# Halves of a batch's queries of 256 and 320 tokens instead of 320 and 256

## The chip, the cores and the metric

The kernel runs on one core of a Trainium2 chip. The metric is the device time of one execution in microseconds, the median of the runs that were timed.

## What is computed

Three layers follow each other. The first is attention with 4 batches, 8 heads, 576 tokens a batch and 64 numbers a head. It has two parts that are added: every query sees the keys less than 4 positions away (local), and the mean of 4 neighbouring queries sees the 144 means of 4 neighbouring keys (pooled), its output being repeated for the 4 tokens:

```python
out_d = sm_attn(q_d, k_d, v_d)               # means of 4 tokens, 144 a batch
out_up = np.repeat(out_d, factor, axis=2)
mask = np.abs(pos[:, None] - pos[None, :]) < factor
...
return (out_up + out_local).astype(np.float32)
```

The second layer is dense, over 2304 tokens of 512 numbers: `h = x @ w_in; g = h * cos(h); x = g @ w_out`, with 2048 hidden numbers. The third routes each token to the best of 8 experts (512 to 1024 to 512 with a relu) and scales by the softmax of the gate.

## The kernel before

**Attention.** A batch's 576 queries are nine tiles of 64. Two heads (a head pair, hp = 0 to 3) are worked on together, one in partitions 0 to 63 and one in 64 to 127. `HALF` (line 72) cuts the 576 queries in two: for each half the first group of 4 tokens, the number of groups, and the groups in one pooled product. So the first half has 80 groups, that is 320 tokens or five tiles, and its pooled queries go in two products of 40; the second has 64 groups, that is 256 tokens or four tiles, in one product of 64. `QROWS` gives the shape in which the queries are loaded.

`queries` (line 152) does one half of one head pair in seven steps, with a `yield` behind each: transposes of the queries (tq, L128, L165 to L169); local scores with a mask and their exponentials p (L178 to L191; a tile of 64 queries sees a window of 70 keys); pooled scores and their exponentials pd (L200 to L207); transposes of p (pt, L214); transposes of pd and, where there is a fifth tile, of its p (ptd, L222 to L229); pooled output (o, L234, L237); local output (L245), the sum of both (xo, L247), and a sink that takes it on. `together` runs several of these generators in turn, one step each. In batch 0 the four head pairs of the first half run together, then the four of the second; in batches 1 to 3 the two halves of each head pair do.

**Handing over.** `first_x` (line 297) is the sink in batch 0: it cuts the tokens of a half at the blocks of 256 and writes each piece as a rounded part xh (L306, ScalarE) and a rest xl (L307; VectorE for the first half, GpSimd for the second) into the blocks x[0] and x[1], and what lies beyond token 512 goes to the DRAM tensor xT through SP's queue (L311). All other batches go through xT (L264 to L282), and `load_x` brings blocks 2 to 8 back.

**The dense layer.** Tokens go in nine blocks of 256. `hidden(i, fp)` (L379) makes 256 hidden numbers of block i, with 24 matmuls of rounded and rest parts, then `h * cos(h)` on ScalarE and VectorE (L385 to L393); `project(i, fp)` (L407) adds them into the block's output. The float64 weights are loaded as words by SP (L329), joined on VectorE (L339 to L343), and split on ScalarE (L348) and GpSimd (L350) by `convert_w`. The weights (fp, 0) are for `hidden`, (fp, 1) for `project`.

**Order.** The program's text gives priorities, and a scheduler plans the order on each engine from them before the run. The first half of batch 0 runs first, with three conversions among its steps; xo is held behind the joining of the last of them by `issue_after`. `hidden(0, 0)` and `hidden(0, 1)` follow. From there a list of slots interleaves the dense layer with the rest of the attention: `marks` gives the step of the attention that is due at each slot. The second half of batch 0 is due by slot 1, ahead of the first hidden of block 1, `(1, 0)`. Steps are counted in yields, and each half has seven.

Of the kernel before, what the change touches and what calls it, by code (L numbers as in the profile page):

```python
# [10 lines left out]
BF16 = mybir.dt.bfloat16  # L11
# [8 lines left out]
P = 128  # L20
# [11 lines left out]
class Kernel:  # L32
# [18 lines left out]
    def constants(self):  # L51
        nc, pool = self.nc, self.const
        self.ident = pool.tile([P, P], F32, name="ident")
        nc.gpsimd.memset(self.ident, 0.0)
        nc.gpsimd.affine_select(out=self.ident, in_=self.ident, compare_op=ALU.not_equal, fill=1.0,
                                base=0, pattern=[[-1, P]], channel_multiplier=1)
        self.ident16 = pool.tile([P, P], BF16, name="ident16")
        nc.gpsimd.tensor_copy(self.ident16, self.ident)
        self.mask = pool.tile([P, 9, 70], BF16, name="mask")
        nc.gpsimd.memset(self.mask, 0.0)  # L60
        for half in range(2):
            for t0, t1, off in ((0, 1, 0), (1, 8, 3), (8, 9, 6)):
                m = self.mask[half * 64:(half + 1) * 64, t0:t1, :]
                pat = [[0, t1 - t0], [-1, 70]]
                nc.gpsimd.affine_select(out=m, in_=m, compare_op=ALU.is_ge, fill=NEG,
                                        base=off + 3, pattern=pat, channel_multiplier=1)
                nc.gpsimd.affine_select(out=m, in_=m, compare_op=ALU.is_ge, fill=NEG,
                                        base=3 - off, pattern=[[0, t1 - t0], [1, 70]], channel_multiplier=-1)

    HALF = ((0, 80, 40), (80, 64, 64))
    QROWS = ((80, 4), (128, 2))
    KROWS = ((96, 3), (96, 3))
    VHALF = ((0, 72), (72, 72))

# [9 lines left out]
    def lane(self, pool, engine, n):  # L86

        qs = []
        for j, (g0, ng, gq) in enumerate(self.HALF):
            qdbd = pool.tile([P, ng // gq, 2, gq], F32, name=f"qdbd{n}_{j}")  # L90
# [25 lines left out]
    def load_windows(self, b, h, j):  # L116

        g0, ng, _ = self.HALF[j]
        first = g0 // 16 + (1 if j == 0 else 0)
# [34 lines left out]
    def queries(self, pool, n, n_, j, qs, raw, hp, kd, kT, vd, vw, sink, behind=None):  # L154

        nc, S = self.nc, self.S
        qdbd = qs[j]
        g0, ng, gq = self.HALF[j]
        nt, nd, t0 = ng // 16, ng // gq, g0 // 16
# [3 lines left out]
        ps = self.psum([P, 320], f"tq_{n_}")  # L163
        self.turn(ps, raw, self.QROWS[j], hp)
        nc.scalar.mul(qT[:, :4 * ng], ps[:, :4 * ng], 0.125)  # L165
        nc.vector.tensor_reduce(out=qd[:, :ng], in_=ps[:, :4 * ng].rearrange("p (g f) -> p g f", f=4), axis=AX.X, op=ALU.add)
        for par in range(2):
# [7 lines left out]
        sm = pool.tile([P, 5], F32, tag="sm", bufs=n, name=f"sm_{n_}")  # L175
        p = pool.tile([P, 5, 70], F32, tag="p", bufs=max(n, 2), name=f"p_{n_}")
        ps = self.psum([P, 5, 70], f"s_{n_}")
        nc.tensor.matmul(ps[:, :nt, :], lhsT=self.ident16, rhs=self.mask[:, t0:t0 + nt, :], start=True, stop=False,  # L178
                         skip_group_check=True)
        for i in range(nt):  # L180
            w0 = min(max(64 * (t0 + i) - 3, 0), S - 70)
            for par in range(2):
                r = slice(64 * par, 64 * par + 64)
                nc.tensor.matmul(ps[r, i, :], lhsT=qT[r, 64 * i:64 * i + 64], rhs=kT[r, w0:w0 + 70],  # L184
                                 start=False, stop=(i == nt - 1), skip_group_check=True)
# [12 lines left out]
        ps = self.psum([P, 2, 144], f"sd_{n_}")  # L198
# [13 lines left out]
        ps = self.psum([70, 4, P], f"pt_{n_}")  # L212
# [4 lines left out]
        ps = self.psum([80, 512], f"ptd_{n_}")  # L217
# [13 lines left out]
        ps = self.psum([P, 512], f"o_{n_}")  # L231
        for kj, (k0, nk) in enumerate(self.VHALF):
            for par in range(2):
                nc.tensor.matmul(ps[64 * par:64 * par + 64, 320:320 + ng].rearrange("p (a b) -> p a b", a=nd), lhsT=vd(kj, par)[:nk],  # L234
                                 rhs=pdT[kj][:, :, gq * par:gq * par + gq], start=(kj == 0), stop=(kj == 1))
# [18 lines left out]
    def attention(self, pool, qs, b, hp):  # L254

        nc, S = self.nc, self.S
        n_ = f"{b}_{hp}"
        ks, vs = [], []
        for j, (r, n) in enumerate(self.KROWS):
            ks.append(pool.tile([P, 4, P], F32, tag="raw", bufs=self.RAWS, name=f"rawk{j}_{n_}"))  # L260
            self.load_rows(ks[j], self.k, b, hp, j * r * n, (r, n))
        for j, (g0, ng) in enumerate(self.VHALF):
            vs.append(pool.tile([P, 512], F32, tag="raw", bufs=self.RAWS, name=f"rawv{j}_{n_}"))
            nc.sync.dma_start(out=vs[j][:ng].rearrange("g (h c) -> g h c", h=2),  # L264
                              in_=self.v[b, 2 * hp:2 * hp + 2, 4 * g0:4 * (g0 + ng), :].rearrange("h (g f) d -> g h (f d)", f=4))
        yield
        for kd, kT in self.keys(pool, 1, ks, None, n_):
            yield
        vd = self.pooled_values(pool, 1, vs, 2, n_, nc.gpsimd)
        yield  # L270
        halves = []
        for j, (g0, ng, _) in enumerate(self.HALF):
            raw = pool.tile([P, 4, P], F32, tag="raw", bufs=self.RAWS, name=f"rawq{j}_{n_}")
            self.load_rows(raw, self.q, b, hp, 4 * g0, self.QROWS[j])
            vw = pool.tile([70, 5, 2, 64], F32, tag="vw", bufs=2, name=f"vw{j}_{n_}")
            edge, e0, i0 = (0, 0, 1) if j == 0 else (3, S - 70, 0)
            nc.sync.dma_start(out=vw[:, edge, :, :], in_=self.v[b, 2 * hp:2 * hp + 2, e0:e0 + 70, :].rearrange("h s d -> s h d"))
            for par in range(2):
                nc.sync.dma_start(out=vw[:, i0:i0 + ng // 16 - 1, par, :], in_=self.load_windows(b, 2 * hp + par, j))

            def sink(x, g0=g0, ng=ng):
                nc.sync.dma_start(out=self.xT[hp * P:(hp + 1) * P, b * S + 4 * g0:b * S + 4 * (g0 + ng)], in_=x[:, :4 * ng])  # L282

            halves.append(self.queries(pool, 2, n_, j, qs, raw, None, kd, kT, lambda kj, par: vd[kj][:, par, :],
                                       lambda i, par, vw=vw: vw[:, i, par, :], sink))
        yield
        yield from self.together(halves, 2)
# [11 lines left out]
    def first_x(self, x, hp, j):  # L299

        nc, TB = self.nc, self.TB
        at, done = 4 * self.HALF[j][0], 0
        while at < 2 * TB and done < 4 * self.HALF[j][1]:
            n = min(TB - at % TB, 4 * self.HALF[j][1] - done)
# [440 lines left out]
    def run(self):  # L745
        nc, tc, E, NT, KD = self.nc, self.tc, self.E, self.NT, self.KD
        S = self.S
# [31 lines left out]
        def load(nm, src, rows=None, j=0):  # L779
            raw[nm, j] = pr.tile([P, 2048], F32, tag="raw", name=f"raw{nm}{j}")  # L780
            if rows is None:
                self.load_pooled(raw[nm, j], src, 0, j)
            else:
                self.load_batch(raw[nm, j], src, 0, j * rows[0] * rows[1], rows)

        def windows(j):
            vw = pp.tile([70, 5, 8, 64], F32, tag="vw", name=f"vw{j}")
            ng = self.HALF[j][1]
            edge, e0, i0 = (0, 0, 1) if j == 0 else (3, S - 70, 0)
            nc.sync.dma_start(out=vw[:, edge, :, :], in_=self.v[0, :, e0:e0 + 70, :].rearrange("h s d -> s h d"))  # L790
            for h in range(8):
                nc.sync.dma_start(out=vw[:, i0:i0 + ng // 16 - 1, h, :], in_=self.load_windows(0, h, j))
            return vw

        for j in range(2):
            load("k", self.k, self.KROWS[j], j)
        load("q", self.q, self.QROWS[0])
        self.constants()
        pool = self.const
# [35 lines left out]
        for hp in range(4):  # L835
            for got in self.keys(pp, 4, [raw["k", j] for j in range(2)], hp, f"0_{hp}"):
                pass
            kv.append(got)
        vw = windows(0)
        for w in early[1:]:  # L840
            self.load_w(*w)
# [4 lines left out]
        def first(hp, j):  # L846
            if j == 0:
                q, at = raw["q", 0], hp
            else:
                q, at = ap.tile([P, 4, P], F32, tag="raw", bufs=self.RAWS, name=f"rawq_{hp}"), None  # L850
                self.load_rows(q, self.q, 0, hp, 4 * self.HALF[1][0], self.QROWS[1])
            yield from self.queries(pp, 4, f"0_{hp}", j, lanes[hp], q, at, *kv[hp],
# [11 lines left out]
        self.hbanks = [psh]  # L864
        self.abanks = [banks, self.psx]
        vw = windows(1)
        raws.close()
        att = ExitStack()
# [200 lines left out]
```

## Time and profile before

| | |
|---|---|
| median of 3 runs | 896.86 us (890.33 to 897.53) |
| profiled execution | 899.56 us, span of its trace 897.4 us |
| TensorE matmul busy | 837.3 us, 93% |
| VectorE busy | 540.8 us, 60% |
| ScalarE busy | 506.9 us, 56% |
| GpSimd busy | 203.1 us, 23% |
| mean granted TensorE clock | 0.956 of 2.4 GHz |

The span runs from the first to the last instruction of the profiled execution; its time has the launch around it as well. A busy share is a mean over the whole span, and stages differ.

### The profile page before, as it was taken

What the parts mean: (1) busy time and instruction counts of PE and PEld (TensorE: products, weight loads), DVE (VectorE), ACT (ScalarE), POOL (GpSimd) and SP (SyncE); (2) the same over time, 40 slices, a digit from 0 to 9 for tenths busy, and PEclk for the clock granted to TensorE, in tenths of its full rate; (3) what the DMA queues carried; (4) which work ended last, traced back from release to release, by engine and by line L of the source; (5) the groups of instructions that cost most, each with busy time, mean ns of one, the idle gap of its engine ahead of it and who ended that gap; (6) DMA issues with size and microseconds to landing.
All of it is one profiled execution on the core that took longest, in us unless ns stands there. A gap on an engine that the chain in (4) does not pass through costs nothing.

```text
span 897.4 us, 16850 instructions
## 1 busy us (share of the span) xinstructions
PE 837.3 (93%) x6114; PEld 724.6 (81%) x6114; DVE 540.8 (60%) x1331; ACT 506.9 (56%) x1278; POOL 203.1 (23%) x296
## 2 busy tenths in 40 slices
PE   6779897999899999899999999999899999999995
PEld 5577776878787888788888989898779888888894
DVE  5874789854634467585574848587455654555420
ACT  4657766777557576656744444475255644545421
POOL 4544345341221222221201010110222022012200
PEclk9579889899989999999999999999999999999998
DMA  9822925223415222332010000052548655455110
GB/s 200 266 70 60 334 67 165 58 69 91 101 42 148 68 56 59 70 80 71 1 37 25 26 25 24 31 160 71 150 133 299 224 174 174 163 171 193 58 37 22
DMA packets 112730, 95.89 MB, mean 107 GB/s; under 512 B 65152, under 2 KB 92876, under 8 KB 112636
## 3 DMA queue, kind: packets, MB, share of 16 engines
q1 hardware_dynamic: 108524, 83.96, 32.0%
q0 software_dynamic: 4112, 10.76, 4.0%
q8 instruction: 50, 0.82, 0.4%
q14 instruction: 44, 0.36, 0.1%
HBM read 81.31 MB, written 13.98 MB: 106 GB/s over the span
## 4 chain that ended last, share of the span: by engine, by line
PE 70%; DMA 8%; DVE 7%; issue 6%; ACT 5%; POOL 3%; SPq 1%; POOLq 0%; DVEq 0%; ACTq 0%
PE h L379 19%; PE acc L407 19%; PE eacc L655 10%; PE eph L636 9%; DMA lists<-tokens,posi 2%; PE s L184 2%; PE o L234 2%; DMA xT<-xo 1%; DMA raw<-in_moe_w_dram 1%; PE sd L200 1%; PE o L245 1%; PE ptd L222 1%; DVE w L343 1%; DMA out_dram<-y,ids 1%; PE tq L128 1%
## 5 line engine op out<-in xcount | busy, mean ns | idle before, releaser
L379 PE MATMUL h<-xh,w 128*128 128x256 f32 x1152 | 236.6, 294 | 8.1 <-POOL w L350 3.6
L379 PEld LDWEIGHTS h<-xh,w 128*128 128x128 f32 x1152 | 190.5, 196 | 12.9 <-POOL w L350 4.2
L407 PE MATMUL acc<-w,gh 128*128 128x512 f32 x576 | 194.9, 412 | 0.0
L379 PE MATMUL h<-xl,w 128*128 128x256 f32 x576 | 167.9, 292 | 1.4 <-DVE xl L307 1.4
L407 PEld LDWEIGHTS acc<-w,gh 128*128 128x128 f32 x576 | 105.2, 192 | 19.9 <-ACT gh L392 0.3
L636 PE MATMUL eph<-exh,w 128*128 128x256 f32 (+5 forms) x512 | 117.8, 306 | 0.0
L407 PE MATMUL acc<-w,gl 128*128 128x512 f32 x288 | 116.8, 406 | 0.4 <-DVE gl L393 0.4
L379 PEld LDWEIGHTS h<-xl,w 128*128 128x128 f32 x576 | 112.7, 196 | 4.0 <-DVE xl L307 1.6
L564 DVE TENSOR_TENSOR w<-raw,w 128x512 fp32r<-128x512 f32 x128 | 83.4, 688 | 32.0 <-ACT w L563 31.4
L655 PE MATMUL eacc<-w,hh 128*128 128x512 f32 (+4 forms) x304 | 99.2, 407 | 1.0 <-ACT hh L644 1.0
L636 PEld LDWEIGHTS eph<-exh,w 128*128 128x128 f32 x512 | 87.8, 190 | 3.3
L563 ACT CAST w<-raw 128x512 fp32r<-128x512 f32 x128 | 73.7, 619 | 28.4 <-DMA raw<-in_moe_w_dram 15.0
L385 ACT ACTIVATE u<-h 128x512 int32<-128x512 f32 x72 | 43.3, 601 | 70.9 <-PE h L379 70.7
L636 PE MATMUL eph<-exl,w 128*128 128x256 f32 (+5 forms) x256 | 78.6, 307 | 0.0
L389 DVE SCALAR_TENSOR_TENSOR u<-u,h 128x512 f32<-128x512 f32 x72 | 49.3, 685 | 48.4 <-ACT u L388 48.0
L386 DVE SCALAR_TENSOR_TENSOR u<-h,u 128x512 f32<-128x512 f32 x72 | 49.3, 685 | 37.7 <-ACT u L385 37.2
L455 DVE SCALAR_TENSOR_TENSOR prod<-row,wgb 128x512 f32<-128x512 f32 x96 | 66.4, 691 | 6.5 <-ACT row L449 5.0
L483 POOL DMA_INDIRECT lists<-tokens,posi x18 | 19.3, 1074 | 210.5 <-DVE posi L480 205.2
L392 ACT CAST gh<-u 128x512 fp32r<-128x512 f32 x72 | 44.8, 622 | 36.7 <-DVE u L389 20.5
L407 PEld LDWEIGHTS acc<-w,gl 128*128 128x128 f32 x288 | 55.0, 191 | 12.4 <-DVE gl L393 0.9
L393 DVE TENSOR_TENSOR gl<-u,gh 128x512 fp32r<-128x512 f32 x72 | 52.0, 723 | 20.6 <-ACT gh L392 20.3
L387 ACT ACTIVATE u<-u 128x512 f32<-128x512 f32 x72 | 45.5, 631 | 30.3 <-DVE u L386 30.1
(178 smaller groups left out, 1442.5 us busy)
## 6 DMA issues: line engine op xcount, KB each, us to landing
raw<-in_moe_w_dram SPq DMA_DIRECT2D x64, 512.0 KB
f<-in_moe_w_in_dram SPq DMA_DIRECT2D x8, 1024.0 KB
f<-in_moe_w_out_dram SPq DMA_DIRECT2D x8, 1024.0 KB
rows<-row SPq DMA_DIRECT2D x9, 520.0 KB
xraw<-xT SPq DMA_DIRECT2D x14, 256.0 KB
rawk<-in_k_dram SPq DMA_DIRECT2D x48, 72.0 KB
rawv<-in_v_dram SPq DMA_DIRECT2D x24, 144.0 KB
vw<-in_v_dram SPq DMA_DIRECT2D x32, 70.0 KB
```

Of the source, the lines that this page charges most:

```text
L379: nc.tensor.matmul(ph[:, fo, :], lhsT=a[:, kk, f], rhs=b[:, kk, :], start=(n == 0), stop=(n == 3 * self.KD - 1))
L386: nc.vector.scalar_tensor_tensor(out=u, in0=hv, scalar=1.0 / (2 * math.pi), in1=turns, op0=ALU.mult, op1=ALU.subtract)
L387: nc.scalar.activation(u, u, AF.Sin, scale=PI)
L389: nc.vector.scalar_tensor_tensor(out=u, in0=u, scalar=1.0, in1=hv, op0=ALU.subtract, op1=ALU.mult, reverse0=True)
L392: nc.scalar.copy(gh, u)
L393: nc.vector.tensor_tensor(out=gl, in0=u, in1=gh.bitcast(F32), op=ALU.subtract)
L407: nc.tensor.matmul(self.acc[i][t], lhsT=a[:, fo, t * P:(t + 1) * P], rhs=b[:, fo, :], start=(f == 0 and n == 0), stop=(f == self.NF - 1 an ...
L455: nc.vector.scalar_tensor_tensor(out=prod, in0=row[:, t, :DM], scalar=1.0, in1=self.spread[e // 2][:, e % 2, :], op0=ALU.mult, op1=ALU.mul ...
L563: nc.scalar.copy(hi, raw[:, sl])
L564: nc.vector.tensor_tensor(out=lo, in0=raw[:, sl], in1=hi.bitcast(F32), op=ALU.subtract)
L636: self.lastmm = nc.tensor.matmul(ph, lhsT=a[:, kk, f % 2 * P:(f % 2 + 1) * P], rhs=b[:, kk, :cols], start=(n == 0), stop=(n == 3 * self.KD ...
L655: self.lastmm = nc.tensor.matmul(self.eacc[w][:m], lhsT=a[:, at * P:at * P + m], rhs=b[:, f % 2, :], start=(f == 0 and n == 0), stop=(f == ...
```

## The change

The two halves change their sizes. The first half of every batch has 64 groups, so 256 tokens, four tiles, one pooled product of 64; the second has 80 groups, 320 tokens, five tiles, two pooled products of 40. The queries' load shapes change places with them. The mask held one pattern for each of the nine tiles, of which the seven inner ones are alike; it now holds six, and a half takes its own from place 0 or 1 on. The window at the end of the sequence stands in place 4 of the second half's five. `first_x` is not edited, but its cuts now fall elsewhere: the first half is block 0 and nothing else, and the second is block 1 and 64 tokens for xT.

```diff
-        self.mask = pool.tile([P, 9, 70], BF16, name="mask")
+        self.mask = pool.tile([P, 6, 70], BF16, name="mask")
...
-            for t0, t1, off in ((0, 1, 0), (1, 8, 3), (8, 9, 6)):
+            for t0, t1, off in ((0, 1, 0), (1, 5, 3), (5, 6, 6)):
...
-    HALF = ((0, 80, 40), (80, 64, 64))
-    QROWS = ((80, 4), (128, 2))
+    HALF = ((0, 64, 64), (64, 80, 40))
+    QROWS = ((128, 2), (80, 4))
...
-        nc.tensor.matmul(ps[:, :nt, :], lhsT=self.ident16, rhs=self.mask[:, t0:t0 + nt, :], start=True, stop=False,
+        nc.tensor.matmul(ps[:, :nt, :], lhsT=self.ident16, rhs=self.mask[:, j:j + nt, :], start=True, stop=False,
...
-            edge, e0, i0 = (0, 0, 1) if j == 0 else (3, S - 70, 0)
+            edge, e0, i0 = (0, 0, 1) if j == 0 else (4, S - 70, 0)
```

The last pair of lines stands twice in the kernel, in `attention` and in `windows`.

## Rows read from the trace of the kernel before

**Rows 1.** Stretches of 20 us: length, then busy us (instructions) of each engine, clock, DMA.

```profile
20.00:40.00 20.00, 13.47 (x112) 9.76 (x112) 18.82 (x50) 14.11 (x61) 8.19 (x9) 0.58 0.97 308
40.00:60.00 20.00, 13.77 (x109) 12.94 (x107) 16.84 (x33) 10.33 (x22) 9.64 (x7) 0.67 0.27 62
...
480.00:500.00 20.00, 20.00 (x132) 17.92 (x131) 12.12 (x31) 10.14 (x17) 2.30 (x2) 1.00 0.01 1
```

**Rows 2.** Chain of waits, 0 to 62 us: start, us, engine, name, line, count.

```profile
14.36 2.42 PE s L184 x40
...
23.97 3.12 ACT p L188 x20
...
44.84 5.78 PE h L379 x25
...
56.13 3.04 POOL w L350
...
60.87 0.43 PE tq L128 x2
```

**Rows 3.** VectorE's timeline: start, us, then the idle time before and its releaser.

```profile
37.41 1.28 DVE L343 SCALAR_TENSOR_TENSOR w<-f,w 128x512 int32<-128x512 int32 x2
39.67 0.49 DVE L247 TENSOR_TENSOR xo<-o,od 128x320 f32<-128x320 f32 x1 [0.97 <-PE o L245]
40.73 0.49 DVE L247 TENSOR_TENSOR xo<-o,od 128x320 f32<-128x320 f32 x1 [0.57 <-PE o L245]
41.80 0.49 DVE L247 TENSOR_TENSOR xo<-o,od 128x320 f32<-128x320 f32 x1 [0.57 <-ACT xh L306]
```

**Rows 4.** Groups by shape, 0 to 60 us: count, busy us, mean ns, idle before.

```profile
L245 PE MATMUL o<-pT,vw 70*64 70x64 f32 x80 | 4.7, 314 | 0.0
...
L222 PE MATMUL ptd<-ident,pd 80*72 80x80 f32 x16 | 3.2, 340 | 0.5 <-ACT pdT L225 0.3
L203 ACT ACTIVATE pd<-sd,mxd 80x144 f32<-80x144 f32 x8 | 2.9, 385 | 0.0
...
L207 DVE TENSOR_SCALAR pd<-pd,smd 80x144 f32<-80x144 f32 x8 | 2.0, 286 | 0.1
...
L228 PE MATMUL ptd<-ident,p 128*70 128x128 f32 x4 | 1.5, 424 | 0.0
...
L204 DVE TENSOR_SCALAR smd<-smd 80x2 f32<-80x2 f32 x4 | 1.3, 328 | 0.0
...
L65 POOL TENSOR_SCALAR_AFFINE_SELECT mask<-mask 64x490 bf16<-64x490 bf16 x2 | 1.3, 633 | 0.0
...
L229 ACT COPY pT<-ptd 70x128 f32<-70x128 f32 x4 | 1.0, 262 | 0.7 <-PE ptd L228 0.5
...
L307 DVE TENSOR_TENSOR xl<-xo,xh 128x64 fp32r<-128x64 f32 x4 | 0.9, 214 | 0.0
```

**Rows 5.** Groups by shape, 60 to 92 us.

```profile
L207 DVE TENSOR_SCALAR pd<-pd,smd 128x144 f32<-128x144 f32 x4 | 1.0, 292 | 0.0
...
L204 DVE TENSOR_SCALAR smd<-smd 128x1 f32<-128x1 f32 x4 | 0.4, 145 | 0.0
```

**Rows 6.** SP's DMA issues in the timeline.

```profile
15.62 8.68 SPq L792 DMA_DIRECT2D vw<-in_v_dram  x8
...
43.17 3.70 SPq L792 DMA_DIRECT2D vw<-in_v_dram  x8
```

**Rows 7.** Chain of waits, 55 to 135 us.

```profile
75.89 1.92 ACT pT L215 x4
...
82.23 3.73 DMA xT<-xo
...
87.59 5.93 PE h L379 x35
```

**Rows 8.** ScalarE's timeline at the start of the second half's exponentials.

```profile
67.57 1.28 ACT L188 ACT_TABLE_LOAD   x1
68.86 0.32 ACT L188 ACTIVATE p<-s,mx 128x70 f32<-128x70 f32 x1
```

More of the change, by code (lines that the diff above doesn't have):

```diff
@@ L788, in windows @@
             ng = self.HALF[j][1]
-            edge, e0, i0 = (0, 0, 1) if j == 0 else (3, S - 70, 0)
+            edge, e0, i0 = (0, 0, 1) if j == 0 else (4, S - 70, 0)
             nc.sync.dma_start(out=vw[:, edge, :, :], in_=self.v[0, :, e0:e0 + 70, :].rearrange("h s d -> s h d"))
```

## The prediction

> **What bounds the kernel now.** I began with the page's busy shares, where TensorE stands far ahead of the others, and with the table by stretches of 20 us. In the middle of the kernel TensorE is busy for 20.00 of 20 us [rows 1], so only two things can move the end: TensorE work that is added or dropped, and time in which TensorE has nothing to do. The sum of TensorE's work hardly changes here, because every batch still has nine tiles of 64 queries; what changes is in which half the fifth tile stands. So I looked for the places where TensorE idles. The same table shows them at the front: 13.47 and 13.77 us busy in the two stretches from 20 to 60 us, at a mean granted clock of 0.58 and 0.67 [rows 1]. Until about 45 us no token of the first dense layer can be multiplied, because its inputs are the output of the first half of batch 0.
>
> The second view is the chain of waits from 0 to 62 us [rows 2]. It runs through TensorE (scores), ScalarE (the exponentials p, then the pooled ones pd), and only at 44.84 us into the first hidden matmuls. VectorE's timeline shows the second route beside it: the conversion of the weight (0, 1) ends there at 37.41 + 1.28 = 38.69 us, and the first sum of local and pooled attention (xo, line 247) starts only 0.97 us later, because TensorE's o of line 245 was not there yet [rows 3]. So at that point TensorE is the later of the two, by 0.97 us.
>
> The last view is the chain after 55 us [rows 7]: the second half of batch 0 is on it too. It ends at 87.59 us, where the second block of tokens starts, and from there on the kernel runs with few holes.
>
> **The change, part by part.** Today's first half (five tiles, pooled queries in two groups of 40) and today's second half (four tiles, one group of 64) change places. So the trace holds the price of either shape already: the forms of 0 to 60 us are those that the second half will have, and the forms of 60 to 92 us those that the first half will have.
>
> *What leaves the front.* (a) Scores: 40 instructions in 2.42 us are 0.06 us each; for the two head pairs in that row 32 remain, so 0.5 us go [rows 2]. (b) ScalarE's p: the row of 3.12 us holds ten exponentials with their readouts, two head pairs of five; two go, 0.62 us [rows 2]. (c) ScalarE's pd: 2.9 us for eight; four remain, since one group replaces two, so 1.45 us go [rows 4]. (d) TensorE's late part: the fifth transposes of line 228 go, 1.5 us busy; 16 of the 80 instructions of line 245 go, 4.7 x 16/80 = 0.94 us; of line 222 eight wider ones replace sixteen; I take 1.0 of its 3.2 us, between 0 (a wide one costs twice a narrow one) and 1.6 (the same) [rows 4]. By TensorE's route that is 0.5 + 0.62 + 1.45 + 1.5 + 0.94 + 1.0 = 6.0 us.
>
> VectorE's route gives less. Its work is conversions, which stay, and small steps, of which line 207 falls from 2.0 to 1.0 us and line 204 from 1.3 to 0.4 [rows 4, 5]: 1.9 us, with (a) 2.4. As xo is queued behind the conversion by the program (issue_after), VectorE decides the first xo after the change: it comes 2.4 us earlier for the work, plus the 0.97 us of waiting that vanishes, 3.4 us in all. Behind it, xo of the second and third head pair wait 0.57 us each today, the one put down to TensorE and the other to ScalarE's cast of the pair before, which itself came late for TensorE [rows 3]; with TensorE 6.0 us earlier these waits go, 1.1 us. First_x then makes one piece a head pair instead of two: four 64-column subtractions of 0.9 us together leave VectorE [rows 4], about two of them ahead of the first block's start, 0.4 us. **Front: 3.4 + 1.1 + 0.4 = 4.9 us gained.** Its bounds are 2.4 (only the work, every wait returns elsewhere) and 6.4 (TensorE's route and the 0.4). I take 4.9, as two of its three waits have a row that names TensorE as the later engine.
>
> The weights must not come later than that. SP spends 8.68 us on the issue of the eight window loads of the first half; the other five weights' loads stand behind them in its queue [rows 6]. Those eight carry three tiles instead of four after the change and the four query loads become two, so the weights move forward with the rest. The smaller mask saves part of 1.3 us of GpSimd, twice [rows 4], hidden by TensorE's transposes of k, which need no mask; if that cover were gone it would be worth at most those 2.6 us.
>
> *What the second half gets.* It runs from 60 to 87 us beside hidden work of the first block. ScalarE goes into its exponentials at 67.57 with a table load of 1.28 us and p at 68.86, and is the chain's engine at 75.89 [rows 7, 8]. It gets four more p of 0.31 us (3.12 / 10 [rows 2]), 1.25; four more pd of 0.36 (2.9 / 8), 1.45; four more copies of line 229, 1.0 us [rows 4]; and TensorE eight more scores for the last head pair's share and the wider pieces of xh and xl, 0.5. **Second half: 4.2 us lost.** Bounds: 2.5, if p (1.25) and the 0.5 disappear under TensorE's projections, which fill it until 75 us [rows 7]; 6.8, with one more pair of table loads (2 x 1.28). I take the sum whole, because ScalarE has no idle time to absorb it after 67.57 and the chain leaves TensorE for ScalarE at 75.89. The second half's loads grow by a quarter: the window loads took 3.70 us of SP's queue from 43.17 us on [rows 6], the queries behind them about as long, so a quarter of both is 1.9 us; the keys of batch 1 are queued behind them. The queries are read at 60.87 [rows 2], some 9 us after SP was done with these loads, so I cost it at nothing; without that cover it is 1.9 us.
>
> What remains as it is: xo has three buffers for four head pairs, so the last pair waits for a store to DRAM, 3.73 us from 82.23 [rows 7]; both halves keep it. In batches 1 to 3 the two halves run together, alternating, and their sums are equal; I cost them at nothing, and bound them by one store wait either way, 3.7 us.
>
> **The sum.** -4.9 + 4.2 = -0.7 us. Against the profiled execution's own 899.56 us that is 898.9; it stands 2.7 us above the median of the three runs, 896.86, so on their scale I predict **896.2 us**. From the bounds: -6.4 + 2.5 = -3.9 and -2.4 + 6.8 = +4.4, with 3.7 either way for the later batches: 889 to 905. The faster rival below ends lower still, so the range goes down by 2 more: 887 to 905. The runs of before, 890.33 to 897.53, also lie within it. A change of under 1%, 9.0 us, can't be told from none.
>
> **The rivals.**
>
> *Slower: the longer second half breaks on ScalarE's tables.* Today the last sine of the first block stands just ahead of the table load at 67.57 and the exponentials follow it without another [rows 8]. If the planner, with front and second half closer together, puts the exponentials' start ahead of that sine, ScalarE switches to sine and back: 2 x 1.28 = 2.57 us. It decides when the scores of the first head pair are ready before hidden (0, 2) ends, and today that hidden is held back by 3.04 us on GpSimd at 56.13 [rows 2], which speaks for it; against it speaks that the hidden's matmuls stand ahead of the scores in TensorE's queue. With a front gain of only 3.4 (the PE waits come back as ScalarE's casts): -3.4 + 4.2 + 2.6 = +3.4, or **900.3 us**; with a store wait more in the later batches, 904; a longer hole of TensorE that drops its clock to half again (the first hidden's 25 matmuls took 5.78 us after such a hole, half of it lost [rows 2]) would bring it to 907.
> The Trainium skill ("ScalarE: Activation LUTs", What ACT_TABLE_LOAD costs) puts a switch at about 2.66 us, load and drain together, so a pair at 5.3 and this rival at +6.1; the trace does not agree: p starts 1.29 us after the load did [rows 8].
>
> *Faster: the second half moves into the hole.* From 56.13 us the chain stands on GpSimd for 3.04 us, until 59.17, while TensorE waits [rows 2]. If the planner now places the transposes and scores of the second half there, the section starts that much sooner: -0.7 - 3.0 = -3.7; if the last pair's store (3.73) is covered as well by hidden work, -7.4: **889 to 893 us**, and 886 with one store wait less in the later batches. Against it: the queries of the second half land late, behind larger window loads, and the order is fixed before the run.
>
> *Nothing at all:* the start of the first block gains and the second block's start loses the same, and the kernel lies within the spread of its own runs: 897 us.
>
> **How the numbers follow.** Forecast (889 to 901) 0.45; nothing 0.10; slower rival 0.22; faster rival 0.23. Only the ends of the two rivals pass 1%: half of each, so faster 0.12, slower 0.11, within 1% 0.77. The range of 887 to 905 leaves about 0.2 out.
>
> **What would show it.** Right: the run of first hidden matmuls that begins at 44.84 us today at 39 to 41 us; line 203 with four exponentials of 128 partitions in the front and eight of 80 behind; xo's first instruction directly behind the conversion; the second block's hidden start near 87 us again. Wrong: the first hidden not earlier than 43 us (then the front term failed); the second block starting before 83 us (faster rival) or after 90 us with a third table load between 60 and 90 us (slower rival); or a difference that arises after 140 us, which none of my terms holds except the bound for the later batches.

## The result, and the profile after

The changed kernel takes **889.01 us** (median of 20 runs, 885.88 to 895.25) against 897.1 us for the kernel before on the same chip (20 runs, 890.33 to 900.68). The ratio is 0.9915, with a 95% interval of 0.9895 to 0.9935: 0.65 to 1.05% faster, some 8 us. The two profiled executions stand further apart than the medians, 885.88 us (span 884.1) against 899.56 us (span 897.4), so the 13.3 us between the two traces contain about 5 us of ordinary spread. Both traces hold the same 6114 matmul instructions of TensorE, which is busy with them for 837.3 us before and 825.1 after. So 12.2 of the 13.3 us are busy time, in which the same work took longer before, at a mean granted clock of 0.956 against 0.973; TensorE's idle time hardly changes (60.1 and 59.0 us).

The first two stretches of [rows 1], with two more (length, busy us of each engine, clock, DMA), of the kernel after:

```profile
20.00:40.00 20.00, 9.62 (x122) 7.15 (x122) 18.70 (x46) 10.46 (x40) 12.25 (x11) 0.68 0.95 301
40.00:60.00 20.00, 14.23 (x75) 13.37 (x76) 18.88 (x27) 9.01 (x16) 7.33 (x6) 0.72 0.33 66
60.00:80.00 20.00, 19.43 (x184) 14.85 (x182) 12.28 (x40) 18.06 (x79) 10.69 (x20) 1.00 0.26 62
...
240.00:260.00 20.00, 19.23 (x171) 16.48 (x172) 10.79 (x36) 14.04 (x30) 6.31 (x11) 1.00 0.22 67
```

The two added stretches, of the kernel before:

```profile
60.00:80.00 20.00, 19.26 (x163) 15.70 (x161) 11.25 (x38) 15.87 (x63) 10.16 (x21) 0.90 0.26 62
...
240.00:260.00 20.00, 17.28 (x108) 15.56 (x107) 8.63 (x34) 10.92 (x34) 4.09 (x7) 0.83 0.26 45
```

The front stays a place where VectorE is full (18.7 and 18.9 of 20 us) and TensorE idles. The new thing is the stretch 240 to 260 us: before, TensorE lost 2.7 us there and ran at a mean clock of 0.83; after, it lost 0.8 us at full clock.

To see where two traces part, I laid them over each other by the runs of `hidden`. Line 379 has 1728 matrix products in the trace, 72 runs of 24, one for each call of `hidden`; I count the runs from 0 and take the start of each run's first product. Runs 0 to 2 are block 0's, run 3 is block 1's first.

| start of run, us | 0 | 2 | 3 | 4 | 18 | 19 | 22 | 71 | end |
|---|---|---|---|---|---|---|---|---|---|
| before | 42.7 | 56.4 | 83.2 | 89.7 | 240.6 | 256.1 | 282.7 | 612.8 | 897.4 |
| after | 37.9 | 54.7 | 84.8 | 89.4 | 236.7 | 247.2 | 272.7 | 601.8 | 884.1 |
| difference | -4.7 | -1.7 | +1.5 | -0.3 | -4.0 | -8.9 | -10.0 | -11.0 | -13.3 |

Where the change was meant to act, the front and the second half of batch 0, hardly anything is left at run 4: -0.3 us. Almost everything arises behind it, and the largest single step, 4.9 us, is between runs 18 and 19: 15.4 us before, 10.5 after. What makes this step so long before is called the hole from here on.

**The hole, read in the trace.** The chain of waits of the kernel before (start, us, what):

```profile
227.91 3.65 DMA xT<-xo
...
231.65 0.06 DVE xo L247
...
236.68 8.47 DMA lists<-tokens,posi
...
246.28 1.39 POOL p L191 x2
...
247.72 0.63 PE pt L214 x4
```

GpSimd's timeline in the same place, before:

```profile
236.68 0.98 POOL L483 DMA_INDIRECT lists<-tokens,posi  x1 [0.30 <-issue]
237.70 0.27 POOL L169 TENSOR_SCALAR qdbd<-qd 64x80 f32<-64x80 f32 x1
245.32 0.88 POOL L169 TENSOR_SCALAR qdbd<-qd 64x80 f32<-64x80 f32 x3 [7.36 <-DMA lists<-tokens,posi]
```

TensorE's transposes of p, before:

```profile
247.72 0.63 PE L214 MATMUL pt<-ident,p 128*70 128x128 f32 x4 [2.72 <-POOL p L191]
```

TensorE's transposes of p, after:

```profile
241.81 0.63 PE L214 MATMUL pt<-ident,p 128*70 128x128 f32 x4 [0.77 <-POOL p L191]
```

Block 0 has just been routed, and GpSimd writes the tokens' places into two lists in DRAM. The second instruction behind these writes, a `qdbd` of an attention pair, carries a wait for both of them in the program, though it reads neither list, so GpSimd stands for 7.36 us. Behind it in GpSimd's queue is that pair's product of p (L191), and TensorE, whose other work runs out at 245.00 us, waits 2.72 us for it. Then the clock falls. Stretches of 4 us, before:

```profile
244.00:248.00 4.00, 1.28 (x12) 1.00 (x11) 1.89 (x3) 0.89 (x3) 2.12 (x5) 1.00 0.29 50
248.00:252.00 4.00, 4.00 (x21) 3.71 (x19) 0.00 (x0) 3.72 (x4) 0.00 (x0) 0.56 0.00 0
252.00:256.00 4.00, 4.00 (x15) 3.22 (x15) 2.18 (x13) 0.42 (x3) 0.00 (x0) 0.58 0.27 105
```

TensorE idled 2.72 us, and then 4 x (1 - 0.56) + 4 x (1 - 0.58) = 3.4 us went to products at or near the lower of the two clock levels, 1.2 GHz. Together 6.1 us. After the change the same wait is 0.77 us and the clock stays at 1.00, which makes 5.3 us less by this estimate, against 4.9 in the table. GpSimd still stands 6.92 us for the lists then; but it issues the second write 5.5 us earlier (at 231.19 us), and TensorE's other work runs out only 4.0 us earlier (at 241.04).

### The profile page after: what moved, and what is told of

It reads as the page before. It is cut to its first block, busy times and chain, and to the rows that moved or that the text cites. A ratio compares the mean times of both kernels' runs of the same rounds, so it can differ in the third digit from the quotient of the medians.

```text
span 884.1 us, 16847 instructions
## 1 busy us (share of the span) xinstructions
PE 825.1 (93%) x6114; PEld 710.8 (80%) x6114; DVE 543.0 (61%) x1327; ACT 510.8 (58%) x1276; POOL 211.7 (24%) x296
## 4 chain that ended last, share of the span: by engine, by line
PE 70%; issue 8%; DVE 8%; DMA 6%; ACT 4%; POOL 3%; SPq 0%; POOLq 0%; DVEq 0%; ACTq 0%
PE acc L407 21%; PE h L379 21%; PE eacc L655 8%; PE eph L636 8%; DMA out_dram<-y,ids 2%; PE s L184 2%; PE o L245 1%; PE pt L214 1%; DVE w L343 1%; DMA rows<-rows,esrc 1%; PE o L234 1%; DVE w L341 1%; DMA raw<-in_moe_w_dram 1%; ACT p L188 1%; PE ptd L222 1%
## 5 line engine op out<-in xcount | busy, mean ns | idle before, releaser
L379 PE MATMUL h<-xh,w 128*128 128x256 f32 x1152 | 231.7, 290 | 9.1 <-DVE u L389 4.6
L379 PEld LDWEIGHTS h<-xh,w 128*128 128x128 f32 x1152 | 187.1, 193 | 13.3 <-issue 4.8
L379 PE MATMUL h<-xl,w 128*128 128x256 f32 x576 | 165.7, 288 | 2.7 <-DVE xl L307 2.4
L379 PEld LDWEIGHTS h<-xl,w 128*128 128x128 f32 x576 | 110.9, 193 | 6.2 <-DVE xl L307 3.2
L393 DVE TENSOR_TENSOR gl<-u,gh 128x512 fp32r<-128x512 f32 x72 | 58.0, 805 | 12.7 <-ACT gh L392 12.0
L689 POOL DMA_INDIRECT out_dram<-y,ids x22 | 22.1, 1004 | 176.6 <-ACT y L688 156.0
```

Source lines behind the costliest of these rows:

```text
L379: nc.tensor.matmul(ph[:, fo, :], lhsT=a[:, kk, f], rhs=b[:, kk, :], start=(n == 0), stop=(n == 3 * self.KD - 1))
L393: nc.vector.tensor_tensor(out=gl, in0=u, in1=gh.bitcast(F32), op=ALU.subtract)
```

## The experiments

At first I took another row of the same chain for the cause. The store `xT<-xo` at 227.91 us stood behind loads in SP's queue, and VectorE's next xo, with its one buffer, waited for it. What ended VectorE's idle time before line 247, 140 to 460 us (us, times), before:

```profile
  DMA xT<-xo: 11.7, 9
```

And after:

```profile
  DMA xT<-xo: 4.8, 3
```

This is theory S, and the first four runs were built on it. Each ratio below is against runs of the kernel before on the same chip.

### The change in parts, and the buffer

e1_later and e2_first give the new halves to batches 1 to 3 alone, or to batch 0 alone; e3 and e4 take the store wait away, before and after the change:

```diff
-    HALF = ((0, 80, 40), (80, 64, 64))
-    QROWS = ((80, 4), (128, 2))
+    HALVES = (((0, 80, 40), (80, 64, 64)), ((0, 64, 64), (64, 80, 40)))
+    QROWSS = (((80, 4), (128, 2)), ((128, 2), (80, 4)))
...
-        g0, ng, gq = self.HALF[j]
+        g0, ng, gq = self.HALVES[b > 0][j]
...
```

(this is e1_later; in e2_first the two entries of each change places, and in both the mask is the changed one). The buffers of e3 and e4:

```diff
-        qT = pool.tile([P, 320], F32, tag="qT", bufs=n, name=f"qT_{n_}")
+        qT = pool.tile([P, 320], F32, tag="qT", bufs=max(n, 3), name=f"qT_{n_}")
...
-        x = pool.tile([P, 320], F32, tag="xo", bufs=max(n - 1, 1), name=f"xo_{n_}")
+        x = pool.tile([P, 320], F32, tag="qT" if n == 2 else "xo", bufs=3, name=f"xo_{n_}")
```

> New halves (256, 320) in batches 1 to 3 alone; batch 0 keeps 320 and 256. Theory S (store wait): the gain of 8 us arises in batches 1 to 3, where the one xo buffer waits for the first half's store; with four tiles first and five second the store lands ahead. Then this is faster than before by 5 to 9 us, and VectorE's waits of xo for the store between 140 and 460 us fall from 11.7 us to about 5. Theory F (front): the gain is batch 0's; then within 2 us of before. Theory P (planner): any new plan moves the time by some us either way and the halves have nothing to do with it; then anything within 8 us, with no relation to the store waits.

Measured: 893.87 us, ratio 0.9973 (0.9943 to 1.0002).

> New halves in batch 0 alone. Theory S: within 3 us of before, since batch 0's second block of tokens starts at the same time and the store waits of batches 1 to 3 stay at about 12 us. Theory F: faster by 6 to 8 us. Theory P: anything within 8 us.

Measured: 899.86 us, 1.0015 (0.9984 to 1.0046).

> The kernel before, with xo of batches 1 to 3 taken from three buffers that it shares with qT, so that the second half's xo need not wait for the first half's store. Theory S: faster than before by 4 to 8 us, store waits of xo after 140 us near 0, and no hole of 2.7 us and half clock near 245 us. Theories F and P: no gain by itself, within 3 us of before (F), or anything (P).

Measured: 887.53 us, 0.9883 (0.9842 to 0.9923), no wait for a store left.

> The changed kernel with the same three shared buffers. Theory S: the change has already hidden most stores, 4.8 us of waits are left, so 0 to 3 us faster than the changed kernel (6 to 11 faster than before), and nearly equal to the kernel before with these buffers. Theory F: the gains of front and buffers add, so the difference to the kernel before with these buffers stays near 8 us. Theory P: anything.

Measured: 891.42 us, 0.9942 (0.9914 to 0.997), no wait for a store left.

F falls: new halves in the first batch alone bring nothing. S looked good in e3, but e4, with as little waiting, is no faster than the changed kernel, and e1, with 2.5 us of it left in two waits, got a third of the gain, with an interval that reaches none. In e1 another wait of the same engine was in the way, at 160 us; GpSimd, then TensorE:

```profile
160.13 4.16 POOL L191 TENSOR_TENSOR p<-p,sm 128x350 f32<-128x350 f32 x1 [0.86 <-DVE smd L204]
```

```profile
164.34 1.07 PE L214 MATMUL pt<-ident,p 128*70 128x128 f32 x4 [3.33 <-POOL p L191]
```

The same product took 0.7 us each at 246 us (1.39 for two, above).

### The store wait taken away in another way, and rivals

e7 issues the store from ScalarE's queue; e8 is e1 with e3's buffers:

```diff
-                nc.sync.dma_start(out=self.xT[hp * P:(hp + 1) * P, b * S + 4 * g0:b * S + 4 * (g0 + ng)], in_=x[:, :4 * ng])
+                nc.scalar.dma_start(out=self.xT[hp * P:(hp + 1) * P, b * S + 4 * g0:b * S + 4 * (g0 + ng)], in_=x[:, :4 * ng])
```

> The kernel before, with the one edit that the store of a half's output (line 282, batches 1 to 3) is issued from ScalarE's queue instead of SyncE's, so that it no longer stands behind the loads of the next pair; halves, buffers and everything else as before. Theory S (the change gained because the second half's output, which has one buffer, waits less for the first half's store: 11.7 us in nine waits between 140 and 460 us before, 4.8 us in three after): the nine waits shrink to the time that a transfer takes, line 247 waits under 5 us in all, PE stays busy between 240 and 260 us (before 17.28 of 20 us, clock 0.83), and the time is 887 to 891. Rival Q (the store's place in the queue is not it: the buffer is held by the transfer itself, 3.65 us in the chain): the waits stay above 8 us and the time at 895 to 898. Rival A: ScalarE, which now stands at each store until VectorE's add is done, hands the time back, waits gone and time 893 to 899.

Measured: 894.84 us, 0.9969 (0.9939 to 0.9998). The waits fell to 1.6 us in three, as S wants, and the time did not follow. TensorE in the hole of e7, and its clock:

```profile
244.06 0.63 PE L214 MATMUL pt<-ident,p 128*70 128x128 f32 x4 [1.95 <-POOL p L191]
```

```profile
248.00:252.00 4.00, 4.00 (x14) 3.39 (x14) 2.19 (x13) 0.50 (x3) 0.00 (x0) 0.50 0.29 113
```

So S falls as the main cause. The store wait and the hole are neighbours in one chain, and e3 had happened to lose both. Rival A hit the time; but in the hole TensorE waits for GpSimd's product, not for ScalarE.

> The new halves in batches 1 to 3 alone (batch 0 keeps 320 and 256), with three buffers for the outputs of those batches, so that no second half waits for a store. The new halves alone gave 893.9 with 2.5 us of such waits left and a hole at 160 us, in which TensorE waits 3.3 us for GpSimd's product of line 191. Theory S alone (the wait for the store is all that matters): 2.5 us less than 893.9 at least, and near the kernel before with the same buffers, 887.5: 886 to 890. Rival G (what kept the new halves in the later batches from their gain is the hole at 160 us, GpSimd's product slowed beside VectorE's weight conversions, which no buffer mends): the hole stays, the time is 891 to 894.

Measured: 890.36 us, 0.9908 (0.9873 to 0.9942), between the two forecasts: the hole at 160 us went with the new order (runs 10 to 14 took 40.8 us, 48.7 in e1), while TensorE's wait for p behind the lists was 1.23 us.

e10 is e1 with the product of batches 1 to 3 on VectorE:

```diff
-        nc.gpsimd.tensor_tensor(out=p[:, :nt, :], in0=p[:, :nt, :], in1=sm[:, :nt].unsqueeze(2).to_broadcast([P, nt, 70]), op=ALU.mult)
+        (nc.vector if n == 2 else nc.gpsimd).tensor_tensor(out=p[:, :nt, :], in0=p[:, :nt, :], in1=sm[:, :nt].unsqueeze(2).to_broadcast([P, nt, 70]), op=ALU.mult)
```

> The new halves in batches 1 to 3 alone, as in e1_later (893.9), with the product of line 191 of those batches on VectorE instead of GpSimd. Theory G (the hole at 160 us, where TensorE waited 3.3 us for a GpSimd product that took about four): the hole goes, h11 to h14 start no later than in the kernel before, and the time falls to 888 to 891. Rival (VectorE is as loaded there, and 24 products of 0.4 to 0.8 us come on top of its conversions): another wait takes the hole's place, 893 to 898.

Measured: 888.07 us, 0.9897 (0.9862 to 0.9931). Both waits for GpSimd's p are gone, runs 10 to 14 take 41.5 us and runs 18 to 19 take 9.6, although VectorE waits 5.5 us for stores, more than in e1. That turned the question to GpSimd (theory L: the loss is TensorE's wait for the product of p that stands behind the list writes).

### The hole taken out of the old kernel, and put into the new one

e12 is e10's edit on the kernel before, with its old halves:

> The kernel before with one edit: in batches 1 to 3 the product of line 191 runs on VectorE instead of GpSimd; halves, buffers and the store's queue as before. Theory L (what before loses and the change gains is the one hole near 245 us: GpSimd stands still for some 7 us behind the two writes of the routing lists, the product of line 191 stands behind that, TensorE waits 2.7 us for it and then runs at half clock): without GpSimd in that path TensorE does not wait there, the stretch from the 18th to the 19th hidden run takes 9.6 to 10.5 us (before 15.5), and the time is 889 to 892, although line 247 still waits 8 to 12 us for the store. Theory S (the wait for the store is what costs): those waits are kept, so 896 to 898. A third outcome (VectorE's 0.4 to 0.7 us per product delays its conversions and opens another hole): the stretch is short and the time still 893 to 897.

Measured: 886.11 us, 0.9884 (0.9845 to 0.9922). TensorE's row in the place of the hole carries no wait:

```profile
241.66 0.60 PE L214 MATMUL pt<-ident,p 128*70 128x128 f32 x4
```

Its stretches there, and what is left of VectorE's wait for stores in e12:

```profile
244.00:248.00 4.00, 4.00 (x29) 3.38 (x29) 2.89 (x18) 3.94 (x7) 0.00 (x0) 1.00 0.22 85
248.00:252.00 4.00, 4.00 (x35) 3.70 (x33) 2.40 (x10) 3.13 (x11) 1.97 (x2) 1.00 0.14 49
```

```profile
  DMA xT<-xo: 7.7, 8
```

The lists still hold GpSimd for 7.20 us, but nothing that TensorE needs soon stands behind. With the 24 products of line 191 in these batches on another engine and the halves untouched, the kernel is as fast as the changed one, and somewhat faster than L had said. Not all of that is the hole: of the 9.1 us between the two traces 5.9 are between runs 18 and 19, and 2.4 between runs 4 and 18.

e13 puts the loss into the changed kernel. The order on TensorE, VectorE, ScalarE and SP is the same as in the changed kernel:

```diff
+        self.filler = pool.tile([P, 128], I32, name="filler")
...
         nc.vector.tensor_copy(posi, pos)
+        if i == 0:
+            for _ in range(10):
+                nc.gpsimd.tensor_copy(self.filler, posi[:, 0:1].to_broadcast([P, 128]))
```

> The changed kernel with ten small copies of GpSimd added around the first routed block's list writes (about 0.25 us each by the 0.26 us of line 169, so 1.5 to 2.5 us in all ahead of the product of line 191); the order of work on the other four engines is the same. Theory L: TensorE's wait there grows from 0.8 to 2.3 to 3.3 us and is long enough for the clock to fall as in the kernel before, so the stretch from the 18th to the 19th hidden run goes from 10.5 to 15 to 16 us and the whole time from 889 to 893 to 895: two microseconds put in, about five lost. Rival (the stretch has slack, or the loss is only what is put in): at most 891.

Measured: 895.21 us, 0.9987 (0.996 to 1.0014). GpSimd, TensorE and the stretches of e13:

```profile
239.69 0.24 POOL L170 TENSOR_SCALAR qdbd<-qd 64x64 f32<-64x64 f32 x1 [5.42 <-DMA lists<-tokens,posi]
240.00 2.43 POOL L484 COPY filler<-posi 128x128 int32<-128x128 int32 x7
...
243.06 1.38 POOL L192 TENSOR_TENSOR p<-p,sm 128x280 f32<-128x280 f32 x2
```

```profile
244.50 0.63 PE L215 MATMUL pt<-ident,p 128*70 128x128 f32 x4 [2.10 <-POOL p L192]
```

```profile
244.00:248.00 4.00, 3.50 (x23) 3.38 (x24) 0.00 (x0) 2.05 (x3) 0.44 (x1) 0.83 0.00 0
248.00:252.00 4.00, 4.00 (x14) 3.00 (x15) 2.08 (x14) 0.47 (x2) 0.00 (x0) 0.50 0.05 19
```

The wait grew from 0.77 to 2.10 us, 1.3 more, and runs 18 to 19 from 10.5 to 14.3 us, 3.8 more: the idle time and 2.5 us behind it, at the lower clock. The wait came out shorter than expected, because three of the copies ran before GpSimd's hold and shortened it (5.42 us). The median rose by 6.2 us, more than expected. In the traces 1.4 us of the rise stand ahead of run 18, which I can't explain, and 1.5 near run 34, where nothing was added. There TensorE stops equally long in both kernels. After, the stop and the stretch behind it:

```profile
363.27 0.51 PE L200 MATMUL sd<-kd,qdbd 128*128 128x144 f32 x2 [2.78 <-POOL qdbd L169]
```

```profile
364.00:368.00 4.00, 4.00 (x36) 3.99 (x35) 2.46 (x9) 1.50 (x4) 1.39 (x2) 1.00 0.03 6
```

The same two in e13:

```profile
368.93 0.51 PE L201 MATMUL sd<-kd,qdbd 128*128 128x144 f32 x2 [2.73 <-POOL qdbd L170]
```

```profile
368.00:372.00 4.00, 3.07 (x16) 3.07 (x17) 1.77 (x7) 0.95 (x6) 2.13 (x5) 0.69 0.05 11
```

So the clock fell behind this stop in e13 and not in the changed kernel, with the same order of work on TensorE. No run shows why.

### The front

e9 is the changed kernel with zeros in place of the first low parts:

```diff
+            if fp < 3 and which == 0:
+                nc.gpsimd.memset(tile[:, 1024 + sl.start:1024 + sl.stop].bitcast(F32), 0.0)
+            else:
...
```

> The changed kernel, in which GpSimd writes zeros in place of the low parts of the first three pairs' first weight tiles (line 350, six instructions of the first conversions): these low parts are left out of the product. VectorE's work in the front is the same, GpSimd reads nothing in SBUF beside it. Theory C (the front gave back what it gained because VectorE's subtractions of line 307 took 0.95 us in the mean and up to 1.4 beside GpSimd's of line 350, against 0.41 alone): line 307 falls to 0.4 to 0.6 us, lines 339 to 343 from 0.65 to 0.81 to about 0.5 to 0.7, the first xo comes 1 to 2 us earlier and TensorE's first run proceeds without the waits of 2.98 and 1.99 us, two to four us earlier in all. Rival (the durations are VectorE's own at that shape): they stay. For the end: if the front sets it (F), 885 to 887; if what the front gains is waited for by the second half (as e2_first says), 887.5 to 890, no different from the changed kernel.

Measured: 883.6 us, 0.986 (0.9813 to 0.9906). Line 307 fell to 0.41 us and the first xo came 1.4 us earlier, as C has it; the first run's two waits stayed (3.25 and 1.75 us), and what came earlier is the third run, for which VectorE's u (line 389) was ready sooner. The time is below the forecast of either theory of the end, nearer to F's.

e15 computes the low parts, on VectorE:

```diff
-            nc.gpsimd.tensor_tensor(out=tile[:, 1024 + sl.start:1024 + sl.stop], in0=t[:, sl].bitcast(F32),
+            (nc.vector if fp < 3 and which == 0 else nc.gpsimd).tensor_tensor(out=tile[:, 1024 + sl.start:1024 + sl.stop], in0=t[:, sl].bitcast(F32),
```

> The changed kernel with the low parts of the first three pairs' first weight tiles (line 350, six instructions) computed on VectorE instead of GpSimd, all else in the same planned order but for a few lines. Theory C (VectorE is slowed in the front by GpSimd's subtractions: with zeros in their place everything from the third hidden run on came 5.5 us earlier): VectorE takes on six subtractions of 0.6 to 0.7 us, four of them ahead of the first xo, which comes 2 to 3 us later, but lines 307 and 339 to 343 run at 0.34 to 0.6 us, and the third hidden run starts 1 to 3 us earlier; 886 to 888. Rival (the added work on VectorE is worth as much as the contention it ends): 888.5 to 892.

Measured: 883.88 us, 0.9869 (0.9825 to 0.9913), 2 us better than C had it. VectorE's groups from 30 to 60 us, after, then e15:

```profile
L307 DVE TENSOR_TENSOR xl<-xo,xh 128x256 fp32r<-128x256 f32 x4 | 3.6, 948 | 0.0
```

```profile
L350 DVE TENSOR_TENSOR w<-w,w 128x512 fp32r<-128x512 f32 x4 | 2.6, 686 | 0.0
...
L307 DVE TENSOR_TENSOR xl<-xo,xh 128x256 fp32r<-128x256 f32 x4 | 1.5, 411 | 0.0
```

Run 2 starts at 49.1 us in e9 and 50.8 in e15, against 54.7 after, and in e9, whose order is that of the changed kernel, the 5.6 us stay unchanged up to run 18 (231.1 against 236.7). So a gain made in the front alone is still there at run 18; e2_first, 0.4 us ahead of the kernel before at run 4, lost 5.1 us between runs 4 and 18, where its order is another. At the end of e9's trace only 1.7 of the 5.6 us are left, most of the rest going between runs 19 and 71 (357.6 us, 354.6 after). By the ratios, which are medians, e9 is some 4.9 us and e15 some 4.1 us below the changed kernel. e15's interval and that of the change just overlap (0.9913 and 0.9895), so it is probably, not certainly, the faster.

> The edit of e15_wl_vec and that of e12_before_p_vec together on the changed kernel: the low parts of the first three weight tiles and the products of line 191 in batches 1 to 3 on VectorE. If C and L are both right the gains add: 1 to 3 us from the front and 0.9 us from the hole at 242 us, 884.5 to 887.5, below the changed kernel. If the order planned for the later batches shifts a wait to another place, as in e1_later, it is 887 to 891.

Measured: 886.8 us, 0.9884 (0.9832 to 0.9937). That is in the range for two gains that add, but above e15, so they don't. Runs 18 to 19 take 9.7 us, but e15 by itself already takes 9.7 there, so the second edit had nothing to mend and only brought another order (runs 4 to 18: 148.8 us, 147.7 in e15). Of the kernels that leave nothing out e15 has the lowest ratio, but its interval overlaps those of e3, e12 and e16.

### All kernels by the same measure

| kernel | ratio | runs 4 to 18, us | runs 18 to 19, us | TensorE's wait for p there, us | VectorE's waits for stores, us |
|---|---|---|---|---|---|
| before | 1 | 150.9 | 15.4 | 2.7 | 11.7 |
| e2_first | 1.0015 | 156.0 | 14.4 | 1.6 | 7.2 |
| e13_fill | 0.9987 | 147.9 | 14.3 | 2.1 | 4.3 |
| e1_later | 0.9973 | 153.1 | 11.8 | 0 | 2.5 |
| e7_store_act | 0.9969 | 150.4 | 14.7 | 2.0 | 1.6 |
| e4_after_xo2 | 0.9942 | 146.2 | 12.3 | 1.2 | 0 |
| after | 0.9915 | 147.2 | 10.5 | 0.8 | 4.8 |
| e8_later_xo2 | 0.9908 | 147.4 | 13.8 | 1.2 | 0 |
| e10_p_vec | 0.9897 | 150.8 | 9.6 | 0 | 5.5 |
| e12_before_p_vec | 0.9884 | 148.5 | 9.5 | 0 | 7.7 |
| e16_wl_p_vec | 0.9884 | 148.8 | 9.7 | 0 | 2.8 |
| e3_before_xo2 | 0.9883 | 146.3 | 9.6 | 0 | 0 |
| e15_wl_vec | 0.9869 | 147.7 | 9.7 | 0 | 3.8 |
| e9_no_low | 0.986 | 147.2 | 9.9 | 0 | 1.9 |

The ratio comes from all runs of a kernel, the other columns from one traced execution, which for the changed kernel and e4 is the fastest of its runs and for e12 the slowest. (In e1 TensorE waits 1.9 us in that stretch for ScalarE's row, line 449, instead.) All kernels with 9.5 to 10.5 us between runs 18 and 19 are below 0.992, and those above it have 11.8 us or more; e8 is the one exception. The last column orders nothing: e7 and e4 hardly wait and are slow, e12 waits 7.7 us and is fast.

## Why the prediction was right or wrong

The forecast of 896.2 us was 7.2 us too high; the time lies in the range of 887 to 905, and "within 1%" held, with 0.85%, at its edge. That the range held is luck: it reached down to 887 for a front of 6.4 us, one store wait less and the faster rival, and the hole, which gave the most, had no term of its own. That a change of under 1% can't be told from none was wrong: the runs put this one at 0.65 to 1.05%. The steps in their order:

**What leaves the front: right for xo, too much for hidden.** The first xo was to come 3.4 us earlier; it came 3.3 us earlier [rows 3], directly behind the conversion, and the two waits of 0.57 us are gone. VectorE's timeline after:

```profile
36.33 1.08 DVE L247 TENSOR_TENSOR xo<-o,od 128x256 f32<-128x256 f32 x3
37.33 1.94 DVE L339 TENSOR_SCALAR w<-f 128x512 int32<-128x512 int32 x2
39.19 3.23 DVE L307 TENSOR_TENSOR xl<-xo,xh 128x256 fp32r<-128x256 f32 x3
...
43.28 0.41 DVE L307 TENSOR_TENSOR xl<-xo,xh 128x256 fp32r<-128x256 f32 x1
...
44.82 0.41 DVE L339 TENSOR_SCALAR w<-f 128x512 int32<-128x512 int32 x1
```

GpSimd's, after:

```profile
34.07 7.73 POOL L350 TENSOR_TENSOR w<-w,w 128x512 fp32r<-128x512 f32 x4 [4.96 <-ACT w L348]
```

The first products of `hidden` start at 37.9 us, 4.7 earlier, but then TensorE waits 1.99 us for xl. The product that stood at 44.84 [rows 2] stands at 40.73, 4.1 earlier, the last one of run 1 is 3.0 earlier, and the first of run 2 only 1.7 of the foreseen 4.9. The chain after, whose row of `hidden` begins three products behind that at 40.73:

```profile
36.42 1.00 DVE xo L247 x3
...
39.27 2.83 DVE xl L307 x2
...
42.14 4.98 PE h L379 x20
...
54.72 4.46 PE h L379 x24
```

The mis-sized part is xl: I moved its instructions forward at their old price, and in their new place three of them run beside GpSimd's subtraction, 1.1 us each (3.23 for three), where the fourth, alone, took 0.41. What VectorE loses beside GpSimd in the whole front, in xl and in the joining of the weights, is 3.9 us or more: with six of GpSimd's subtractions on VectorE itself (e15), run 2 starts at 50.8 us instead of 54.7. The Trainium skill ("SBUF — State Buffer", SBUF: two separate sides) says that VectorE and GpSimd share a pair of SBUF ports, which a VectorE operation with two SBUF inputs and a GpSimd operation that reads SBUF take from each other for a whole instruction. Lines 307 and 350 are such a pair, and these rows agree.

**What the second half gets: right in its rows.** Foreseen were 4.2 us; from the start of run 2 to that of run 3 it is 26.9 us before and 30.1 after, 3.2. Where the count begins matters, since before, but not after, TensorE stopped within run 2 for GpSimd's w:

```profile
59.22 0.80 PE L379 MATMUL h<-xh,w 128*128 128x256 f32 x2 [1.62 <-POOL w L350]
```

Counted from the last product of run 2 (63.44 us before, 58.91 after) to run 4 it is 4.2 us. This row also sets a reading of the prediction right: of the 3.04 us for which the chain stands on GpSimd from 56.13 us [rows 2], TensorE waited 1.62 and worked in the others. ScalarE's groups from 60 to 92 us, after:

```profile
L188 ACT ACTIVATE p<-s,mx 128x70 f32<-128x70 f32 x20 | 6.0, 364 | 0.0
...
L203 ACT ACTIVATE pd<-sd,mxd 80x144 f32<-80x144 f32 x8 | 2.9, 438 | 0.0
```

The four more p cost 1.2 us (4.8 us for sixteen before; 1.25 foreseen) and the pooled ones 1.3 (1.6 for four before; 1.45 foreseen). The table is loaded once, as in [rows 8], so the slower rival did not occur; nor did the second half move into the gap at 56 us. SP took 6.63 us for the window loads that took 3.70 [rows 6], and nothing waited for them. Block 1's long run in the chain begins at 88.49 us instead of 87.59 [rows 7]:

```profile
88.49 3.93 PE h L379 x31
```

**The sum of these two** was to be -0.7 us; run 4 shows -0.3. Up to there the sum was right; how much of it is front and how much second half depends on the product at which they are parted.

**What failed** is the step "In batches 1 to 3 the two halves run together, alternating, and their sums are equal; I cost them at nothing, and bound them by one store wait either way, 3.7 us." Equal sums say nothing about waits, and the bound was taken from the wrong wait. The largest piece of the gain is the hole between runs 18 and 19: 4.9 us in the traces. With the wait gone from the old kernel, the time falls by as much as with the change (e12, where the hole is 5.9 of 9.1 us between the traces); with a wait put back and the order untouched, the gain is gone (e13, where it is 3.8 of 7.4 us). Its price is 2.7 us of idle time plus 3.4 us of clock. The second part fell under neither of the "only two things" that the prediction let move the end, work and idle time. The chain of the kernel before shows the wait plainly at 236 to 248 us; I worked from the chain only to 135 us. The prediction did name the sign of this mistake, a difference that arises after 140 us.

**What stays open.** Why the new halves shorten this wait: the routing of block 0 and the pair's p fall otherwise in the planned order, which differs in many places between most of these kernels, and no run isolates one step of it. So theory P, that any new plan moves the time and the halves have nothing to do with it, isn't refuted: with new halves in a part of the batches (e1, e2) the stretch from run 18 to 19 took 11.8 and 14.4 us. The store wait has some part in it, since it delays the routing in the chain above; e7 gives 0.3% for it, with an interval that almost reaches none. And of the 13.3 us between the traces 4.0 ahead of run 18, 2.1 between runs 19 and 71 and 2.3 in the experts' part belong to no cause that I tested; about 5 us of that is the spread of the two profiled executions. The 4.0 are mostly busy time at a lower clock: from 89.7 to 240.6 us TensorE is busy for 136.0 us before, at a mean of 0.93, and from 89.4 to 236.7 for 132.3 us after, at 0.95.

## What to carry to other kernels

When a scheduler plans the order anew, an edit with equal sums can still move a wait somewhere else, so look through the whole trace of before for waits that stand just short of being covered, and price each with the clock that it may cost: in e13 1.3 us more idle time cost 3.8. TensorE's products at the lower clock count as busy, so look at the clock beside the busy share. A wait that is in an engine's queue delays whatever stands behind it; moving a small product off GpSimd, out from behind the list writes, was worth as much as the whole change (0.9884 and 0.9915, with intervals that overlap), and it was one word. Before you credit a wait that vanished together with the time, take it away alone, in two ways: the buffer (e3) agreed with a theory that the queue (e7) then refuted.

## What the runs showed of the hardware that was not expected

VectorE's work in the front depends on what GpSimd does in the same moment: in the changed kernel line 339 took 0.97 us beside GpSimd's subtraction (37.33, 1.94 for two) and 0.41 without it. Giving VectorE six more subtractions of 0.69 us made it finish earlier. And TensorE's clock made a good part of the cost of a short stop, but the length of the stop alone does not tell when. Behind stops of 1.95 (e7), 2.10 (e13) and 2.72 us (before) stands a stretch of 4 us at 0.50 to 0.56, and behind one of 1.23 us in e8 a stretch at 0.50 too. The 0.77 us of the changed kernel left the clock at 1.00; but so did its stop of 2.78 us at 363 us, and this one of e1, with 1.00 in the stretches from 244 to 252 us:

```profile
245.58 1.14 PE L434 MATMUL x2t<-ident,row 128*128 128x128 f32 x8 [1.89 <-ACT row L449]
```
